# Moving the plain couple of a gated attention and max-out kernel from the end of batch 0 to the start of batch 1

## The chip, the cores and the metric

The kernel runs on one core of a Trainium2 chip. The metric is the device time of one execution in microseconds (us), lower is better. Engines: PE is TensorE, DVE is VectorE, ACT is ScalarE, POOL is GpSimd (it issues the plain loads and most stores), SP is SyncE (it issues the transposing DMAs).

## The reference

Eight batches of 3072 tokens; `u` and `v` have 256 columns, `z` has 64. The output of the first half is the input `x` of the second.

```
scores = (1/S) * z @ z.T                  # per batch, symmetric
attn   = max(scores, 0) ** 2
x      = u * (attn @ v)
out    = max(x @ w1, x @ w2) @ w_out      # 1024 hidden columns
```

## The kernel before

**Tiles.** The 3072 rows of a batch are 24 tiles of 128, six groups of four tiles. `A[b, g, k]` is the block of attn between group g and group k: 128 partitions x 2048 bf16, 512 KB, in one of 28 slots. Two groups are a couple, so a batch has couples 0, 1, 2; the program numbers couples through the batches: i = 2 is batch 0's last couple, i = 3 batch 1's first, i = 4 batch 1's second.

**Scores.** A score pair (`score_pair`, L204) is two matmuls of 64 rows (L218), two Relus on ACT (L231) and a square on DVE (L237, L239); two pairs fill one block. attn is symmetric, so only blocks with k >= g are computed; the block (k, g) is made from (g, k) by `mirror` (L268): one transposing DMA on SP (L270). `z` comes transposed in `zT`: `load_z` (POOL, L136), two copies on DVE (L143), a transposing DMA on SP (L144, `turn_z`). `u` comes by `load_u` (POOL, L188) and is transposed by `turn_u` (SP, L194).

**attn @ v.** The four groups of batch 0 that come first (couples 0 and 1) are done one by one (L286). From i = 2 a couple's work is a list of steps of two matmuls (L898), one on each half of PE's rows, with score pairs of later blocks spread between the steps. A couple is done in one of two ways:

- *Plain*: 96 steps; every matmul reads a block of attn and `v` as they are. `PLAIN_COUPLES` names the couple and the order of its three block columns o.
- *By 7 products* (a Strassen form): 84 steps. It needs sums of attn blocks beforehand, for each o of `SUPERS[c]`: S1 = A21 + A22 (L338), S2 = S1 - A11 (L342), S3 = A11 - A21 (L346), and once per batch and o four sums of `v` pieces (`combine_v`, L174 to L177, one of them in place), all on DVE. Products P1 and P6 come first (steps 0 to 11, the first three o's in turn, four steps each), then P7 beside X11 (steps 12 to 23). P6 reads S2, P7 reads S3.

A11, A12 are the blocks of the couple's first group g, A21, A22 those of g + 1. For batch 0's last couple (groups 4, 5) and o = 0 that is A21 = A[0,5,0], A22 = A[0,5,1]: both are mirrors.

**Second half.** `ff` (L443) does the max-out part of one group: hidden products (L448), then output products (L462, L471), stores from POOL (L484). After the steps of couple i, `second(i - 1, ...)` runs `ff` for the two groups of the couple before; while PE does that, a list of tasks is issued on the other engines: the gates (L432, `x = u * ...` of the couple that has just ended) and, ahead of a couple by 7 products, its sums. The sequence of PE is therefore: steps of i = 2, ff of couple 1, steps of i = 3, ff of couple 2, and so on; the `ff` of couple 0 stands ahead of i = 2.

**Order of the queues.** All engines run the program's order, written by hand; no instruction of POOL or SP waits for a "step" of PE as such: it waits only for its data and its buffer, and for what stands ahead of it on its engine. For i = 2, 3, 4 there are plans of their own (L847 to L870): at which step loads and transposes are put into the queues. In batch 0 the mirrors of groups 0 and 1 into groups 3 to 5 are held back (list `later`) and issued during groups 1 to 3; SP's last seven mirrors ahead of i = 2 are, in order, those that make (5,2), (4,0), (4,1), (4,3), (5,0), (5,1), (5,3), and behind them stands the transpose of z(1), piece 1.

Of the kernel before, what the change touches and what calls it, by code (L numbers as in the profile page):

```python
# [11 lines left out]
def kernel(  # L12
# [23 lines left out]
    G = 4  # L36
    GW = G * P
    NG = NT // G
# [4 lines left out]
    NSLOTS = 28  # L43
    AFTER = mybir.DependencyInfo(mybir.DependencyClass.Sync, mybir.DependencyReason.DATA)
    PLAIN = 4
    PLAIN_COUPLES = {2: (2, 1, 0)}
    DIRECT = ((0, 5, 4),)
    KEEP = 5, 2
    SUPERS = (1, 0, 2), (2, 1, 0), (0, 2, 1)
# [18 lines left out]
    def by_tile(x):  # L68
        return x.rearrange("(p t) d -> p t d", t=NT)
# [35 lines left out]
    def z_at(b, t):  # L105
        piece, k = divmod(t, 2 * G)
        return (NC * b + piece) % 4 * 2 * G + k
# [32 lines left out]
    def turn_z(b, piece):  # L140
        t = zpool.tile([P, 2 * G, 2, dqk], bf16, name="zd")
        for h in range(2):
            nc.vector.tensor_copy(t[:, :, h, :], zn[b, piece])  # L143
        nc.sync.dma_start_transpose(  # L144
            zT[:, ds(z_at(b, piece * 2 * G), 2 * G), :], t.rearrange("p t h d -> p (t h d)")
        )
# [20 lines left out]
    def combine_v(b, piece):  # L167
        w = vp[b, piece]
        b11, b12 = w[:, 0:G, 0:P], w[:, 0:G, P:D]
        b21, b22 = w[:, G : 2 * G, 0:P], w[:, G : 2 * G, P:D]  # L170
        t = tpool.tile([P, 3, G, P], bf16, name="vt")
        t1, t2, t3, t4 = vt[b, piece] = b12, t[:, 0], t[:, 1], t[:, 2]
        return [
            lambda: nc.vector.tensor_sub(t3, b22, b12),  # L174
            lambda: nc.vector.tensor_sub(t1, b12, b11),
            lambda: nc.vector.tensor_sub(t2, b22, t1),
            lambda: nc.vector.tensor_sub(t4, b21, t2),  # L177
        ]
# [5 lines left out]
    def load_u(b, g):  # L184
        un[b, g] = unat.tile([P, G, D], bf16, name="un")
        step = 2 if b or g > 1 else G
        for k in range(0, G, step):
            nc.gpsimd.dma_start(  # L188
                out=un[b, g][:, ds(k, step), :], in_=by_tile(u[b])[:, ds(g * G + k, step), :]
            )  # L190
# [10 lines left out]
    A = {}  # L201
# [66 lines left out]
    def mirror(b, g, blk):  # L268
        t = Block(turned=True)
        nc.sync.dma_start_transpose(  # L270
            t.ap.rearrange("p (k r) -> p k r", r=P), A[b, g, blk].ap
        )
        A[b, blk, g] = t
        A[b, g, blk].release(after=COOL)
# [220 lines left out]
    pairs, pair_at = [], {}  # L495
# [17 lines left out]
    per_batch = (len(pairs) - 2 * len(DIRECT)) // B  # L513

    done = 0
# [39 lines left out]
    def need(b, g, n):  # L555
        most = pair_at[b, g, 2 * g]
        for t in range(n + 1):
            if t // G >= g:
                most = max(most, pair_at[b, g, t // 2] + 1)
        return most  # L560

    with tc.manual_schedule():
# [50 lines left out]
        for i in range(PLAIN):  # L613
            b, g = groups[i]
# [3 lines left out]
            for slot, (n, dc) in enumerate(steps_of(i)):  # L618
                tick += 1
                k = need(b, g, n)  # L620
# [16 lines left out]
                if i in (1, 2) and n in (5, 8):  # L637
                    k = n // 8
# [55 lines left out]
        def second(i, tasks, sums=None):  # L694

            b, c = couples[i]
            tasks = list(tasks)
            places = {(1, 0): 1, (1, 3): 1, (2, 0): 1, (2, 1): 1, (2, 2): 1, (2, 3): 1}

            def hook(stage, n):  # L700
                for _ in range(places.get((stage, n), 0)):
                    if tasks:
                        tasks.pop(0)()

            nonlocal tick
            for q in range(2):
                g = 2 * c + q
                ff(b, g, xTs.pop((b, g)), hook=hook)
                tick += 32
            while tasks:  # L710
                tasks.pop(0)()

        def prepared(i, gates):

            b, c = couples[i]
            for o in range(NC):
                assert all(
                    pair_at[b, min(q, k), 2 * max(q, k) + 1] < done
                    for q in (2 * c, 2 * c + 1)
                    for k in (2 * o, 2 * o + 1)  # L720
                ), (i, done)
            for x in list(to_mirror):
                if x[0] == b and x[2] // 2 == c:
                    to_mirror.remove(x)
                    mirror(*x)
            if i in PLAIN_COUPLES:
                return {}, list(gates)
            tasks = []
            for o in SUPERS[c]:
                if (b, o) not in vt:  # L730
                    tasks += combine_v(b, o)
            forms, sums = prepare(b, c)
            first, *others = [x[:2] for x in sums]
            tasks = gates[:KD] + first + gates[KD:] + tasks + sum(others, [])
            return forms, tasks + [x[2] for x in sums]

        b, g = groups[PLAIN - 1]
        sums = drain(acc, range(KD), copy=nc.vector.tensor_copy)
        forms, tasks = prepared(PLAIN // 2, gate(b, g, sums))
        second(  # L740
            PLAIN // 2 - 2,
            [lambda: turn_z(1, 2)]
            + tasks
            + [lambda: None] * 3
            + [lambda g=g: load_u(0, g) for g in (4, 5)],
        )

        for i in range(PLAIN // 2, len(couples)):
            b, c = couples[i]
            q1, q2 = 2 * c, 2 * c + 1  # L750
            target = min(2 * len(DIRECT) + (b + 1) * per_batch + (-6, 8, 22)[c], len(pairs))
            steps, ends, marks, waits = steps_of_couple(
                b, c, forms, supers=PLAIN_COUPLES.get(i)
            )
# [7 lines left out]
            for f in forms.values():  # L762
                for name, n in (("A11", 1), ("A12", 2), ("A21", 1), ("A22", 1), ("S1", 1)):
                    f[name].quota = 2 * G * n
            plain = i in PLAIN_COUPLES
            if plain:
                for q in (q1, q2):
                    for k in range(NG):
                        A[b, q, k].quota = 4 * G
            for pair in steps:  # L770
                for x in pair:
                    left[x[0]] = left.get(x[0], 0) + 1
# [74 lines left out]
            if i == 2:  # L847
                plan = [
                    (1, turn_u, 0, 4),
                    (4, turn_u, 0, 5),  # L850
                    *((17 + 8 * k, load_v, 1, k // 2, k % 2 * G, G) for k in range(6)),
                ]
            if i == 3:
                plan = [
                    (2, load_u, 1, 0),
                    (6, load_u, 1, 1),
                    (14, load_z, 2, 0),
                    (18, load_z, 2, 1),
                    (22, turn_u, 1, 0),
                    (26, turn_u, 1, 1),  # L860
                    (66, turn_z, 2, 0),
                    (len(steps), load_u, 1, 2),
                    (len(steps), load_u, 1, 3),
                ]
# [11 lines left out]
            for s, pair in enumerate(steps):  # L876
                while halves_done and halves_done[0][0] <= s:
                    _, name, mm = halves_done.pop(0)
                    relays[name] = nc.scalar.nop()
                    tc.add_manual_dep(relays[name].ins, mm.ins.name, AFTER, reason="half done")  # L880
                tick += 1
                flush(tick)
                mirror_ready((b, c), KEEP[s > 36])
                asked += len(at_step.get(s, ()))
                while asked and len(due) < 3 and (
                    at_hand() or pairs[done][2] % 2 or len(steps) - s < 8 * asked
                ):
                    emit_pair(wait=8)
                    asked -= 1
                for do in events.get(s, ()):  # L890
                    do()
                for half, (name, w, blk, j) in enumerate(pair):
                    rows = ds(half * R, R)
                    if name not in acc:
                        acc[name] = acc_tile((PLAIN_BANK if plain else BANK)[name])
                    a = blk()
                    left[name] -= 1
                    mm = nc.tensor.matmul(  # L898
                        a.out(acc[name]),
                        w()[rows],  # L900
                        a.moving(rows, j),
                        start=name not in opened,
                        stop=left[name] == 0,
                    )
                    opened[name] = True
                    if (s, half) in marks:
                        halves_done.append((s + (2 if plain else G), marks[s, half], mm))
                    if (s, half) in waits:
                        relay = relays[waits[s, half]]
                        tc.add_manual_dep(mm.ins, relay.ins.name, AFTER, reason="half done")  # L910
                    a.quota -= 1
                    if not a.quota:
                        a.release()
# [11 lines left out]
            if i + 1 < len(couples):  # L925
                forms, tasks = prepared(i + 1, gates)
            else:
                tasks = gates
            second(i - 1, tasks)
        b, c = couples[-1]  # L930
# [31 lines left out]
```

## Time and profile before

| | us |
|---|---|
| median of 7 runs (lowest, highest) | 918.12 (913.64, 923.65) |
| the profiled execution, its own time | 915.91 |
| its span, first to last instruction | 914.1 |
| ff of couple 0 | 68.1 to 83.9 |
| i = 2, plain, with 22 score pairs | 83.9 to 109.4 |
| ff of couple 1 | 109.4 to 125.4 |
| i = 3, by 7 products, with 14 pairs | 125.4 to 146.3 |
| ff of couple 2 | 146.3 to 162.0 |
| i = 4, by 7 products, with 14 pairs | 162.0 to 185.4 |
| the same couple of the next batch (i = 7) | 274.8 to 295.5 |

Times in views are from the span's start. A line of groups or of the timeline has the engine, the source line, the operation, what it writes and reads, and how often; brackets give idle time before it and what ended it. In the waits, the numbers are total us, times, and the longest.

### The profile page before, as it was taken

What the parts mean: (1) busy time and instruction counts of PE and PEld (TensorE: products, weight loads), DVE (VectorE), ACT (ScalarE), POOL (GpSimd) and SP (SyncE); (2) the same over time, 40 slices, a digit from 0 to 9 for tenths busy, and PEclk for the clock granted to TensorE, in tenths of its full rate; (3) what the DMA queues carried; (4) which work ended last, traced back from release to release, by engine and by line L of the source; (5) the groups of instructions that cost most, each with busy time, mean ns of one, the idle gap of its engine ahead of it and who ended that gap; (6) DMA issues with size and microseconds to landing.
All of it is one profiled execution on the core that took longest, in us unless ns stands there. A gap on an engine that the chain in (4) does not pass through costs nothing.

```text
span 914.1 us, 19379 instructions
## 1 busy us (share of the span) xinstructions
PE 899.8 (98%) x7478; PEld 519.3 (57%) x7526; DVE 722.8 (79%) x1094; ACT 602.0 (66%) x1192; POOL 160.7 (18%) x303
## 2 busy tenths in 40 slices
PE   9899999899999999999999999999999999999998
PEld 4456465464565655655556656566465564655655
DVE  6582689778997799887997979979799788995640
ACT  7787966567666676666666666766766667673445
POOL 4102021211202121111213022030220212101000
PEclk9999999999999999999999999999999999999999
DMA  9999999999999896999979998799988989987201
GB/s 180 178 191 201 119 209 173 149 171 165 186 170 148 176 185 127 181 173 157 188 126 200 157 164 174 130 186 170 163 175 138 193 158 173 163 156 147 74 24 69
DMA packets 396556, 145.60 MB, mean 159 GB/s; under 512 B 361904, under 2 KB 387632, under 8 KB 396464
## 3 DMA queue, kind: packets, MB, share of 16 engines
q1 hardware_dynamic: 359040, 91.79, 64.8%
q0 software_dynamic: 37424, 52.58, 32.6%
q8 instruction: 58, 0.95, 0.4%
q14 instruction: 34, 0.28, 0.1%
HBM read 59.77 MB, written 25.17 MB: 93 GB/s over the span
## 4 chain that ended last, share of the span: by engine, by line
PE 95%; DMA 3%; DVE 1%; issue 1%; ACT 0%; ACTq 0%
PE acc L898 43%; PE o_ps L471 18%; PE d_ps L448 18%; PE s_ps L218 7%; PE o_ps L462 5%; PE acc L286 3%; DMA zT<-zd 2%; DMA blk<-blk 1%; DVE blk L239 0%; PE acc L591 0%; PE tpz L125 0%; PE w2o_ps L680 0%; ACT r_sb L231 0%; DVE w_sb L663 0%; DVE xT L432 0%
## 5 line engine op out<-in xcount | busy, mean ns | idle before, releaser
L898 PE MATMUL acc<-blk,v_sb 64*128 64x512 bf16 x2208 | 450.5, 376 | 0.0
L231 ACT ACTIVATE r_sb<-s_ps 128x512 bf16<-128x512 f32 (+3 forms) x672 | 336.0, 559 | 126.5 <-PE s_ps L218 82.9
L898 PE MATMUL acc<-blk,vt 64*128 64x512 bf16 x1512 | 364.1, 376 | 0.0
L898 PEld LDWEIGHTS <-v_sb 64*128 64x128 bf16 x2208 | 176.3, 94 | 135.3 <-issue 5.7
L239 DVE TENSOR_TENSOR blk<-r_sb 128x1024 bf16<-128x1024 bf16 x257 | 172.4, 688 | 93.9 <-ACT r_sb L231 93.2
L455 ACT ACTIVATE g_sb<-d_ps 128x512 bf16<-128x512 f32 x384 | 193.3, 630 | 28.2 <-PE acc L898 17.7
L471 PE MATMUL o_ps<-w_out_sb,g_sb 128*128 128x256 bf16 x1536 | 175.5, 273 | 0.0
L898 PEld LDWEIGHTS <-vt 64*128 64x128 bf16 x1512 | 139.2, 94 | 62.2
L448 PE MATMUL d_ps<-xT,w_sb 128*128 128x512 bf16 x720 | 167.6, 379 | 2.6 <-issue 0.2
L471 PEld LDWEIGHTS <-g_sb 128*128 128x128 bf16 x1536 | 150.3, 98 | 17.4
L483 ACT COPY o_sb<-o_ps 128x512 f32<-128x512 f32 (+1 forms) x98 | 56.3, 577 | 132.5 <-PE o_ps L471 132.5
L484 POOL DMA_DIRECT2D out_dram<-o_sb x88 | 48.1, 547 | 529.6 <-ACT o_sb L483 529.6
L775 DVE TENSOR_TENSOR h_sb<-h_sb,acc 128x512 f32<-128x512 f32 x168 | 109.4, 682 | 28.3 <-ACT h_sb L779 20.9
L218 PE MATMUL s_ps<-zT 64*128 64x512 bf16 (+3 forms) x676 | 126.6, 359 | 2.5 <-DMA zT<-zd 2.5
L448 PEld LDWEIGHTS <-w_sb 128*128 128x128 bf16 x768 | 73.3, 98 | 89.4 <-issue 9.5
L342 DVE TENSOR_TENSOR blk<-blk,blk 128x2048 bf16<-128x2048 bf16 x63 | 77.2, 1225 | 5.6 <-DMA blk<-blk 3.5
L338 DVE TENSOR_TENSOR blk<-blk,blk 128x2048 bf16<-128x2048 bf16 x63 | 76.7, 1218 | 0.0
L790 DVE TENSOR_TENSOR blk<-blk,blk 128x2048 bf16<-128x2048 bf16 x63 | 76.6, 1218 | 0.0
L346 DVE TENSOR_TENSOR blk<-blk,blk 128x2048 bf16<-128x2048 bf16 x63 | 73.3, 1218 | 2.9 <-DMA blk<-blk 2.9
L188 POOL DMA_DIRECT2D un<-in_u_dram x94 | 50.5, 563 | 87.2 <-DMA uT<-un 84.2
L432 DVE SCALAR_TENSOR_TENSOR xT<-h_sb,uT 128x512 bf16<-128x512 f32 x96 | 62.0, 684 | 4.3 <-PE o_ps L462 4.3
L237 DVE TENSOR_TENSOR blk<-r_sb 128x512 bf16<-128x512 bf16 (+3 forms) x162 | 46.5, 324 | 19.7 <-ACT r_sb L231 18.6
(48 smaller groups left out, 358.8 us busy)
## 6 DMA issues: line engine op xcount, KB each, us to landing
out_dram<-o_sb POOLq DMA_DIRECT2D x88, 256.0 KB, 3.7
un<-in_u_dram POOLq DMA_DIRECT2D x92, 128.0 KB, 5.2
v_sb<-in_v_dram POOLq DMA_DIRECT2D x74, 128.0 KB, 5.7
blk<-blk SPq DMA_TRANSPOSE x240, 4.9
v_sb<-in_v_dram POOLq DMA_DIRECT2D x11, 256.0 KB, 13.3
zn<-in_z_dram POOLq DMA_DIRECT2D x21, 128.0 KB, 4.3
out_dram<-o_sb SPq DMA_DIRECT2D x6, 256.0 KB, 2.0
blk<-in_moe_w_dram POOLq DMA_DIRECT2D x2, 512.0 KB, 7.5
```

The source lines that it names most:

```text
L218: nc.tensor.matmul(s_ps[h][:, lo[h] :], zT[rows, z_at(b, blk * G + tiles[h]), :], zT[rows, q + lo[h] // P : q + G, :].rearrange("p t c -> ...
L231: nc.scalar.activation(o, s, AF.Relu)
L239: nc.vector.tensor_mul(a[:, k : k + 2, :], r, r)
L338: nc.vector.tensor_add(*alike(f["S1"], f["A21"], f["A22"]))
L342: nc.vector.tensor_sub(*alike(f["S2"], f["S1"], f["A11"]))
L346: nc.vector.tensor_sub(*alike(f["S3"], f["A11"], f["A21"]))
L448: nc.tensor.matmul(d_ps, w15_sb[:, kc, ts(nb, P)], xT[:, kc, :], start=(kc == 0), stop=(kc == KD - 1),)
L455: nc.scalar.activation(g_sb[:, nb, :], d_ps, AF.Relu)
L471: nc.tensor.matmul(o_ps[t // 2][:, t % 2, :], g_sb[:, nb, ts(t, P)], w_out_sb[:, nb, :], start=False, stop=(nb == KF - 1 and t % 2 == 1),)
L775: nc.vector.tensor_add(out, a, b_)
L790: nc.vector.tensor_sub(f["A12"].ap, f["A12"].ap, f["S2"].ap)
L898: mm = nc.tensor.matmul(a.out(acc[name]), w()[rows], a.moving(rows, j), start=name not in opened, stop=left[name] == 0,)
```

## The change

Couple i = 2 is done by 7 products, with 14 score pairs beside it (`ahead`), and i = 3 plain, with 22. The sums for i = 2 are issued as tasks during the `ff` of couple 0, and batch 0's `combine_v` with them; batch 1's `combine_v` moves from the `ff` ahead of i = 3 to the one ahead of i = 4. `load_u(0, 4)` and `load_u(0, 5)` go from the end of the `ff` of couple 0 to its second and fourth task. `turn_z(1, 2)` goes from that `ff` to step 40 of i = 2. Four of the six loads of v(1) are put at steps 26 to 56 of i = 2 instead of 17 to 41, the last two behind its end instead of at 49 and 57. u(1, 0) and u(1, 1) are loaded and turned some 20 steps sooner. A plain couple may start while the blocks of its last column are still to come.

```diff
-    PLAIN_COUPLES = {2: (2, 1, 0)}
+    PLAIN_COUPLES = {3: (0, 1, 2)}
...
-                ), (i, done)
+                ) or (i in PLAIN_COUPLES and o == PLAIN_COUPLES[i][-1]), (i, done)
...
-        second(
-            PLAIN // 2 - 2,
-            [lambda: turn_z(1, 2)]
-            + tasks
-            + [lambda: None] * 3
-            + [lambda g=g: load_u(0, g) for g in (4, 5)],
-        )
+        for n, g in ((1, 4), (3, 5)):
+            tasks[n] = lambda do=tasks[n], g=g: (do(), load_u(0, g))
+        second(PLAIN // 2 - 2, tasks)
...
-            target = min(2 * len(DIRECT) + (b + 1) * per_batch + (-6, 8, 22)[c], len(pairs))
+            ahead = 14 if i == 2 else (-6, 8, 22)[c]
+            target = min(2 * len(DIRECT) + (b + 1) * per_batch + ahead, len(pairs))
...
             if i == 2:
                 plan = [
                     (1, turn_u, 0, 4),
                     (4, turn_u, 0, 5),
-                    *((17 + 8 * k, load_v, 1, k // 2, k % 2 * G, G) for k in range(6)),
+                    (40, turn_z, 1, 2),
+                    *((26 + 10 * k, load_v, 1, k // 2, k % 2 * G, G) for k in range(4)),
+                    (70, load_u, 1, 0),
+                    (76, load_u, 1, 1),
+                    (len(steps), load_v, 1, 2, 0, G),
+                    (len(steps), load_v, 1, 2, G, G),
                 ]
             if i == 3:
                 plan = [
-                    (2, load_u, 1, 0),
-                    (6, load_u, 1, 1),
+                    (1, turn_u, 1, 0),
+                    (4, turn_u, 1, 1),
                     (14, load_z, 2, 0),
                     (18, load_z, 2, 1),
-                    (22, turn_u, 1, 0),
-                    (26, turn_u, 1, 1),
                     (66, turn_z, 2, 0),
                     (len(steps), load_u, 1, 2),
                     (len(steps), load_u, 1, 3),
                 ]
```

What is left out of the diff counts the uses of a plain couple's blocks when they are first read instead of ahead of the couple.

## The prediction

> **What bounds the kernel now.** I read the page first (busy time, then the chain that ended last), then the waits, then a table by stage.
>
> ```profile
> PE 899.8 (98%) x7478; PEld 519.3 (57%) x7526; DVE 722.8 (79%) x1094; ACT 602.0 (66%) x1192; POOL 160.7 (18%) x303
> ...
> PE 95%; DMA 3%; DVE 1%; issue 1%; ACT 0%; ACTq 0%
> ```
>
> PE is busy 98% of the span and is 95% of the chain, so time can only be won where PE stands still or by less work on PE. The waits of PE show the two places where it stands still for long:
>
> ```profile
> PE acc L286 <- DMA blk<-blk: 2.8, 1, 2.8
> PE s_ps L218 <- DMA zT<-zd: 2.5, 1, 2.5
> ```
>
> The first is at 37.2 us, ahead of everything that the change touches. The second is in i = 4. The table by stage (length, then busy time of PE, PEld, DVE, ACT, POOL with counts, then PE's clock, DMA share, GB/s) finds nothing else:
>
> ```profile
> 68.10:83.90 15.80, 15.70 (x114) 10.91 (x116) 2.61 (x6) 10.08 (x20) 3.80 (x7) 1.00 1.12 198
> 83.90:109.40 25.50, 25.50 (x237) 11.35 (x236) 14.54 (x21) 24.23 (x45) 3.77 (x7) 1.00 1.36 131
> 109.40:125.40 16.00, 15.89 (x114) 10.90 (x116) 15.43 (x25) 10.72 (x22) 1.65 (x3) 1.00 1.18 215
> 162.00:185.40 23.40, 20.87 (x198) 10.59 (x198) 17.64 (x37) 13.60 (x30) 5.38 (x10) 1.00 1.30 146
> 274.80:295.50 20.70, 20.70 (x198) 11.68 (x197) 14.82 (x32) 13.52 (x30) 5.34 (x10) 1.00 1.24 151
> ```
>
> The plain couple with its 22 pairs runs without a hole (25.50 of 25.50), though ACT is busy for 24.23 of it. i = 4 takes 2.7 us more than its sister in the next batch (last line). The ff of couple 1 is 0.2 longer than later ones (15.9 against 15.7). **So from 68 us on there are 2.7 us to win at most.**
>
> **PE's work.** Nothing is added or removed: i = 2 loses 24 matmuls and 8 pairs (16 matmuls), i = 3 gains the same. A stage by 7 products with 14 full pairs takes 21.3 us elsewhere (i = 5, 201.1 to 222.4), the plain one 25.5; their sum stays. Cost 0. Beside the plain i = 3 stand ACT's 44 Relus, as now beside i = 2 without a hole. Cost 0.
>
> **The sums for i = 2: the main term.** In the ff of couple 0 DVE now does 2.61 us of work. It gets S1, S2, S3 for three o's and batch 0's 12 sums of v. The same list stands ahead of i = 6, a couple by 7 products without late inputs:
>
> ```profile
> 225.88 1.22 DVE L338 TENSOR_TENSOR blk<-blk,blk 128x2048 bf16<-128x2048 bf16 x1
> ...
> 228.28 1.28 DVE L432 SCALAR_TENSOR_TENSOR xT<-h_sb,uT 128x512 bf16<-128x512 f32 x2
> 229.48 0.41 DVE L174 TENSOR_TENSOR vt<-v_sb 128x512 bf16<-128x512 bf16 x1
> ...
> 235.87 1.23 DVE L342 TENSOR_TENSOR blk<-blk,blk 128x2048 bf16<-128x2048 bf16 x1
> ...
> 239.41 3.49 DVE L346 TENSOR_TENSOR blk<-blk,blk 128x2048 bf16<-128x2048 bf16 x3
> 242.81 0.68 DVE L239 TENSOR_TENSOR blk<-r_sb 128x1024 bf16<-128x1024 bf16 x1
> ```
>
> From the first S1 to the end of the last S3 it takes 242.81 - 225.88 = 16.93, less two gates (1.20) that i = 2 doesn't have there: **15.7 us in one row**, and DVE takes it in order. There the last S3 is needed at step 20: 24 slots (20 steps, 4 pairs) of 0.217 us (21.26 us / 98 slots of i = 5) after 238.1, at 243.3; it has 0.5 us to spare.
>
> When can the first S1 of i = 2 start? It reads A[0,5,0] and A[0,5,1]. The second is SP's sixth mirror of the last seven, the one at 71.7 (that line of SP's, then its time to landing):
>
> ```profile
> L270 SPq DMA_TRANSPOSE blk<-blk x1: 2422/2422/2422, 71.7 to 71.7; - x1
> ...
> DMA to landing us min/median/max: 5.0/5.0/5.0
> ```
>
> It lands at 76.8. The two gates ahead (L432) end at 73.9, so DVE then waits, and all sums behind wait with it. Last S3: 76.8 + 15.7 = 92.5. PE wants it at step 20: 83.85 + 5.2 = 89.1. **PE waits 3.4 us** (1.8 of it at step 4, where S2 of the second o ends 9.9 after the first S1). In the kernel before, the plain order (2, 1, 0) read these mirrors last.
>
> **The u loads run into those mirrors.** u(0, 4) and u(0, 5), four loads of 128 KB, wait only for buffers that are free by 60.5, and stand right behind POOL's z load of 64.25. So they start near 65 instead of at 77.5, beside the mirrors of 63 to 77. Below: nothing, if SP's pace and not the DMA engines hold these mirrors; a gain is excluded, as SP's first 25 entries are the same in both kernels. Above: the same four loads now stand beside two zT transposes, with two stores, and these land after
>
> ```profile
> DMA to landing us min/median/max: 9.1/9.7/10.4
> ```
>
> instead of the 4.4 median of zT: up to 6.0 later. The loads are half of those bytes (512 KB, the stores 512 KB), which would make 2.7; the loads turn fp32 into bf16 and so read twice as much, and I take 3.5, between the two. **+3.5 (0 to 6.0).**
>
> PE's hole at step 4 becomes 5.3 us. After the 2.83 us hole at 37.2 the granted clock was 0.70 in 40 to 42 and 0.50 in 42 to 44 us, some 3.2 us at half speed, worth 1.6. But DVE's chain paces PE up to step 20 anyway: **+0.5 (0 to 1.6)**. The Trainium skill, "TensorE: Matmul & The Clock Gate", "What's actually happening", speaks against the change here: half rate after an idle window of about 3.4 us, windows running free of the kernel. By that rule a 1.8 us hole is safe and a 5.3 us one may not be; the row shows that 2.83 us was enough, so the row decides, and by the page alone the term would be the same or nothing.
>
> **The stall in i = 4.** PE wants piece 1 of z(2) 17.5 us into the couple (179.5 - 162.0). Its transpose was issued 4.3 in and took 15.9 to land, behind two uT transposes and beside the loads of v(2) and u. The issue comes 1.1 later in the changed kernel: batch 1's 12 sums of v (5.1 us) move into the ff of couple 2, where S3 now ends 18.3 after its start and in the ff with such sums 20.1. That delay itself costs PE nothing, as the ff of couple 1 shows: S3 ended at 129.5 and PE had no hole. The two uT transposes can go earlier, since SP has fewer mirrors piled up (8 blocks fewer beside i = 2). Landing after 10.4 (the slowest zT beside loads above): 15.8 in, no wait, gain 2.5. After 15.9 again: 21.3 in, wait 3.8, loss 1.3. I take **-2.0 (-2.5 to +1.3)**, nearer the first, because the pile ahead is smaller.
>
> **The rest.** u(0, 4) and u(0, 5) land before 80 and their transposes start before the v loads; now these landed 16 and 22 us late, the second at 110.1, and ff of couple 1 was 0.2 long: **-0.2**. z(1)'s last turn (two copies of 0.29 and a DMA) leaves SP at 79.4 for step 40; its first reader is a pair of i = 3: 0, with 15 us of ff as cover; without cover it would be a wait like the 2.5 above. Four of the six v(1) loads don't move at all: POOL doesn't wait for steps, they still stand right behind the stores of ff 0, at 85.4. The last two wait for i = 2's last matmul, since they overwrite batch 0's piece; the stores of ff 1 queue behind them, but the first is ready 7 us later (75.3 against 68.1 in ff 0), and their reader is step 64 of i = 3, some 30 us on. Their landings now are 13 to 17 us: 0. A plain i = 3 reads its last column at step 64; those 8 pairs are done by step 40: 0.
>
> **Sum:** 3.4 + 3.5 + 0.5 - 2.0 - 0.2 = **+5.2 us**. On the profiled execution's own 915.9 (span 914.1 and 1.8 around it) that is 921.1. The median of the runs is 2.2 higher, 918.1; what they have more is not in this profile, and I add the same 5.2 to it: **923.3 us**.
>
> **Rivals.**
>
> *The loads don't hurt* (delay 0 to 1, no loss of clock). For it: SP's mirrors go out back to back from 58.5, so SP may be the limit. Against: they take 1.8 to 3.6 us of SP each, and the 3.6 is the one beside the z load. 3.4 + 0.5 - 2.5 - 0.2 = +1.2: 919.3.
>
> *Not slower: the mirror is there in time.* Without other traffic SP issues a mirror in 1.94 (189.9 us). Six at that pace from 58.5 put the sixth at 68.2, landing at 73.2, ahead of the gates' end at 73.9, the point from which DVE never waits. Then S3 ends at 89.6, PE waits 0.6: 0.6 - 2.5 - 0.2 = -2.1: 916.0. Against: six in a row were slower in the profile, and the loads come on top.
>
> *Worse: the slow stretch moves.* From 85 to 110 us, beside v loads, uT took 16 and 22 us. If loads and mirrors near 66 fall into that, the delay is the full 6.0 and the clock's 1.6, and i = 4 keeps its stall: 3.4 + 6.0 + 1.6 = +11.0: 929.1. Against: it needs the larger v loads.
>
> *It doesn't do what it says*: that holds for four of the v loads, as shown; its price is in the sums.
>
> **Chances.** Forecast 0.62, loads that don't hurt 0.22, mirror in time 0.09, worse 0.07. 0.5% is 4.6 us, about what a measurement of this kernel can tell from no change. Of the forecast's 0.62, 0.50 lies above it; with the worst case, slower 0.57. Faster needs the second rival and more: 0.04. Same: the remaining 0.39. Range: from the second rival, 916.0, to all upper ends, 3.4 + 6.0 + 1.6 + 1.3 = 12.3: 930.4; I write 916 to 930.
>
> **What would show it.** The profile after: PE waiting for DVE (L342, L346) in the first 20 steps of i = 2; DVE idle from 73.9 until a blk DMA lands, near 80; the u loads near 65; i = 2 at 27 to 29 us instead of 21.3; i = 4 at 20.7 to 21.3 instead of 23.4. I am wrong if DVE's first S1 starts before 75, if the mirrors keep their times beside the u loads, or if i = 4 keeps its wait.

## The result, and the profile after

The changed kernel took 922.95 us (median of 26 runs, 921.08 to 931.17) against 917.0 for the kernel before on the same chips (61 runs, 909.18 to 932.14): a ratio of 1.0087, with a 95% interval of 1.0066 to 1.0107. The forecast was 923.3, made on a median of 918.12. The profiled execution took 923.88 (span 922.1), 8.0 us more than the one of before.

First the page: the busy times, and the chain that ended last, which now has DVE in it with 4%.

```profile
PE 904.3 (98%) x7478; PEld 527.7 (57%) x7526; DVE 727.4 (79%) x1106; ACT 601.4 (65%) x1192; POOL 161.0 (17%) x303
...
PE 92%; DVE 4%; DMA 2%; issue 1%; ACT 0%; ACTq 0%; DVEq 0%
```

The waits (total us, times, longest) give the place. The zT wait of 2.5 is gone; in its stead PE waits for S2, and DVE for a mirror.

```profile
DVE blk L338 <- DMA blk<-blk: 6.6, 2, 5.4
...
PE acc L286 <- DMA blk<-blk: 4.4, 1, 4.4
PE acc L896 <- DVE blk L342: 4.1, 1, 4.1
```

The table by stage, with the same columns as before (ff of couple 0, i = 2, ff of couple 1, i = 3 and, after the ff of couple 2, i = 4):

```profile
70.30:86.00 15.70, 15.60 (x112) 10.84 (x111) 6.47 (x11) 10.09 (x20) 1.65 (x3) 1.00 1.19 206
86.00:114.90 28.90, 24.77 (x197) 11.47 (x196) 26.14 (x38) 16.02 (x30) 5.87 (x11) 0.88 1.24 144
114.90:130.60 15.70, 15.60 (x111) 10.87 (x112) 4.92 (x9) 9.71 (x19) 1.65 (x3) 1.00 1.17 131
130.60:156.00 25.40, 25.40 (x238) 19.02 (x236) 14.53 (x27) 22.53 (x46) 3.75 (x7) 1.00 1.25 170
171.80:193.40 21.60, 21.48 (x198) 11.01 (x198) 20.27 (x39) 13.50 (x30) 5.34 (x10) 1.00 1.21 178
```

The plain stage has no hole in its new place (25.40 of 25.40). i = 2 takes 28.9, where the same couple of batch 1 (i = 5) takes 21.26: an excess of 7.6, partly hole (24.77 busy of 28.90), partly clock (0.88). From i = 5 on the two traces agree. Measured between starts of PE's stages, the way from ff of couple 0 to i = 5 grew from 132.97 to 138.85: **+5.9**. The other 2.1 of the 8.0 lie ahead of ff of couple 0 (70.28 against 68.12), where PE's instructions are the same in both kernels: the wait for a mirror at L286 was 4.4 instead of 2.8, with more half clock behind it. That is spread from run to run, not the change: in the profiles of after and of the versions built on it, ff of couple 0 begins anywhere between 64.3 and 77.1.

DVE's timeline shows the chain (start, length, instruction, idle time before it):

```profile
74.81 1.29 DVE L432 SCALAR_TENSOR_TENSOR xT<-h_sb,uT 128x512 bf16<-128x512 f32 x2 [3.73 <-PE o_ps L462]
81.47 1.22 DVE L338 TENSOR_TENSOR blk<-blk,blk 128x2048 bf16<-128x2048 bf16 x1 [5.37 <-DMA blk<-blk]
...
90.26 1.23 DVE L342 TENSOR_TENSOR blk<-blk,blk 128x2048 bf16<-128x2048 bf16 x1
...
93.79 3.49 DVE L346 TENSOR_TENSOR blk<-blk,blk 128x2048 bf16<-128x2048 bf16 x3
97.20 1.89 DVE L239 TENSOR_TENSOR blk<-r_sb 128x1024 bf16<-128x1024 bf16 x3
```

The gates end at 76.1, DVE stands idle for 5.37 us, and the first S1 starts when the mirror has landed. From there to the end of the last S3 it is 97.20 - 81.47 = 15.73. The mirror is the one that SP issued at 76.6:

```profile
L270 SPq DMA_TRANSPOSE blk<-blk x1: 1923/1923/1923, 76.6 to 76.6; - x1
...
  DVE blk L338: 5.4, 1
...
DMA to landing us min/median/max: 4.8/4.8/4.8
```

Its own 4.8 us to landing is ordinary; what made it late is that SP came to it late, since the mirrors ahead of it were slow: (4,3), issued at 67.7, took 9.1 us to land, against 4.6 in before. The DMA view of 60 to 80 us, for before and then for after, shows what lay beside them (packets, MB, share of the 16 engines' time; software_dynamic is POOL's queue):

```profile
q1 hardware_dynamic: 14390, 3.63, 104.5%
q0 software_dynamic: 259, 0.54, 11.0%
```

```profile
q1 hardware_dynamic: 12642, 3.19, 93.5%
q0 software_dynamic: 720, 0.66, 26.0%
```

The u loads add 15% of 20 us to POOL's share, 3.0 us of all engines, and the transposes move 12% less in the same time. That this is the cause is left to e12.

Last, PE's first instruction after the hole, and the clock behind it (the column after the five engines):

```profile
91.53 0.58 PE L896 MATMUL acc<-blk,vt 64*128 64x512 bf16 x1 [4.05 <-DVE blk L342]
```

```profile
90.00:94.00 4.00, 2.39 (x12) 0.87 (x13) 3.93 (x5) 0.96 (x2) 1.06 (x2) 0.62 1.16 117
94.00:98.00 4.00, 4.00 (x22) 1.59 (x23) 4.00 (x5) 1.21 (x3) 0.00 (x0) 0.53 1.29 64
```

By the clock records it was half from 90.97 to 97.80, 6.83 us.

### The profile page after: what moved, and what is told of

The parts are those of the page before. It is cut to its first block, busy times and chain, and to the rows that moved or that the text cites. A ratio compares the mean times of both kernels' runs of the same rounds, so it can differ in the third digit from the quotient of the medians.

```text
span 922.1 us, 19389 instructions
## 1 busy us (share of the span) xinstructions
PE 904.3 (98%) x7478; PEld 527.7 (57%) x7526; DVE 727.4 (79%) x1106; ACT 601.4 (65%) x1192; POOL 161.0 (17%) x303
## 4 chain that ended last, share of the span: by engine, by line
PE 92%; DVE 4%; DMA 2%; issue 1%; ACT 0%; ACTq 0%; DVEq 0%
PE acc L896 44%; PE o_ps L471 17%; PE d_ps L448 17%; PE s_ps L218 7%; PE o_ps L462 4%; PE acc L286 3%; DMA blk<-blk 2%; DVE blk L338 1%; DVE blk L342 1%; DVE blk L239 0%; DVE xT L432 0%; PE acc L591 0%; DVE vt L174 0%; DVE v_sb L175 0%; DVE vt L176 0%
## 5 line engine op out<-in xcount | busy, mean ns | idle before, releaser
L896 PEld LDWEIGHTS <-v_sb 64*128 64x128 bf16 x2208 | 183.1, 94 | 134.1 <-issue 14.3
L218 PE MATMUL s_ps<-zT 64*128 64x512 bf16 (+3 forms) x676 | 133.0, 361 | 0.2 <-DVE zT L130 0.2
L783 DVE TENSOR_TENSOR blk<-blk,blk 128x2048 bf16<-128x2048 bf16 x63 | 76.6, 1218 | 0.1
L346 DVE TENSOR_TENSOR blk<-blk,blk 128x2048 bf16<-128x2048 bf16 x63 | 73.3, 1219 | 1.7 <-DMA blk<-blk 1.7
L218 PEld LDWEIGHTS <-zT 64*128 64x128 bf16 x676 | 39.3, 95 | 37.2 <-issue 1.3
```

The source lines that it names most:

```text
L218: nc.tensor.matmul(s_ps[h][:, lo[h] :], zT[rows, z_at(b, blk * G + tiles[h]), :], zT[rows, q + lo[h] // P : q + G, :].rearrange("p t c -> ...
L346: nc.vector.tensor_sub(*alike(f["S3"], f["A11"], f["A21"]))
L783: nc.vector.tensor_sub(f["A12"].ap, f["A12"].ap, f["S2"].ap)
L896: mm = nc.tensor.matmul(a.out(acc[name]), w()[rows], a.moving(rows, j), start=name not in opened, stop=left[name] == 0,)
```

## The experiments

**Theory.** The end of i = 2 is set by the landing of mirror (5,1) and the sums queued behind it on DVE, and u loads beside the mirrors make that landing later. Let D be the time from the start of ff of couple 0 to that landing. Then the excess of i = 2 over 21.26 should be D + (sums behind it) - 20.9, where 20.9 = 15.7 of ff + 5.2 of 24 slots; clock comes on top. **Rivals:** the amount of DVE work in the ff; the half clock; loads that are hidden anyway.

The profiles, in one table (us; the lateness is the formula's):

| kernel | D | sums behind | lateness | excess measured | half clock in i = 2 |
|---|---|---|---|---|---|
| after | 11.1 | 15.7 | 5.9 | 7.6 | 6.83 |
| e1, order of o | 16.4 | 8.2 | 3.7 | 3.9 | none |
| e2, u later | 6.9 | 15.7 | 1.7 | 2.0 | none |
| e3, PE kept busy | 12.5 | 15.7 | 7.3 | 7.6 | none |
| e4, v sums first | 11.1 | 10.6 | 0.8 | 1.5 | none |
| e8, PE delayed | 9.5 | 15.7 | 4.3 | 5.5 | 3.41 |
| e12, u behind the stores | 9.1 | 15.7 | 3.9 | 4.3 | 3.41 |

**e1: the order of the block columns.** Batch 0's last couple takes o = 2 first, whose sums don't need mirror (5,1).

```diff
-        for o in SUPERS[c]:
+        for o in (2, 0, 1) if b == 0 else SUPERS[c]:
```

> The changed kernel, with the sums of batch 0's last couple in the order o = 2, 0, 1 instead of 0, 2, 1, so that DVE begins with a block column that needs no mirror. Theory (DVE waits for a late mirror with everything behind it): the first S1 starts right behind the gates, 4.5 us after the first output product of that ff or some 6 us after the ff's start, the last S3 ends 15.7 us later, 21.5 after the ff's start, and is wanted at 20.9: i = 2 takes 21.3 + 0.6 = 21.9 us (21.3 to 23) instead of 28.9, with no stretch at half clock; the execution gets 6 to 7 us shorter than the changed kernel, some 916. Rival (the sheer amount of DVE work, 12 more sums and 9 block sums, doesn't fit into this ff): the amount is the same, i = 2 stays at 27 to 29.

918.74 us, ratio 1.0055 (1.0017 to 1.0094). i = 2 fell to 25.18, in full clock, though (5,1) landed 16.4 us after the start of ff: fewer sums stood behind it. That is over the 21.3 to 23 expected, since the mirror landed 5.3 later after that start than in after; the lateness accounts for 3.7 of the excess of 3.9. But i = 4 took 24.88: the transpose of z(2), piece 1, took 14.4 us to land, and PE waited 2.4 for it. The gain in i = 4 isn't safe.

**e2: the u loads later**, beside the seventh and eighth task.

```diff
-        for n, g in ((1, 4), (3, 5)):
+        for n, g in ((6, 4), (7, 5)):
```

> The changed kernel, with the loads of u(0,4) and u(0,5) put back to where the kernel before has them (behind the first two stores of ff 0). Theory (these loads delay the mirrors by some 2.4 us): the mirror that the first S1 waits for lands 8.7 us after the start of ff 0 instead of 11.1, the hole before step 20 is 3.5 instead of 6.0, and with a shorter hole the half clock lasts 0 to 3.4 us instead of 6.8: i = 2 takes 24.8 to 26.5 instead of 28.9. Rival (the mirrors go at SP's own pace, the later landing was the z load or chance): i = 2 stays at 28 to 29.

919.97 us, 1.0069 (1.0018 to 1.0119). i = 2 took 23.25, less than the 24.8 to 26.5 expected, but this profile had a hole of 11.4 us in its opening, so that D was 6.9 partly for that reason. It can't price the loads alone; e12 does.

**e3: PE kept busy in the hole**, by 18 matmuls that nothing reads, ahead of step 4 of i = 2.

```diff
+                if i == 2 and s == 4:
+                    fill = mm_psum.tile([P, GW], fp32, name="fill", tag="mm")
+                    for n in range(18):
+                        nc.tensor.matmul(
+                            fill, w15_sb[:, 0, :P], w15_sb[:, 1, :GW], start=True, stop=True
+                        )
```

> The changed kernel, with 18 matmuls of 128 x 512 that nobody reads on PE ahead of step 4 of i = 2, 3.9 us of work, so that PE isn't idle while it waits there. Theory (1.7 us of the 7.6 us that i = 2 is too long are half clock after the idle hole): no granted clock under 0.9 in i = 2, and i = 2 takes 27.0 to 27.4 instead of 28.9. Rival (DVE's chain sets the pace all along, the clock costs nothing): 28.7 to 29.

922.61 us, 1.0116 (1.0068 to 1.0164). The clock of i = 2 stayed full, and the stage was no shorter, since the mirror landed 1.4 us later than in after:

```profile
85.60:114.50 28.90, 26.59 (x215) 12.57 (x216) 27.46 (x42) 15.96 (x30) 5.90 (x11) 1.00 0.96 151
```

So my expected length was missed, with the measured one in the rival's range, and the lateness explains it (7.3 of 7.6). Half clock isn't the main cause.

**e4: the v sums first.** The 12 sums of v go ahead of the gates and of S1, into the time in which DVE waits for the mirror. The amount of DVE work is unchanged.

```diff
-            tasks = gates[:KD] + first + gates[KD:] + tasks + sum(others, [])
+            if b == 0:
+                tasks = tasks + gates + first + sum(others, [])
+            else:
+                tasks = gates[:KD] + first + gates[KD:] + tasks + sum(others, [])
```

> The changed kernel, with batch 0's 12 sums of v taken ahead of the gates and of the block sums, into time in which DVE waits. The mirror stays as late as it is. Theory: behind the mirror stand 15.7 - 5.1 = 10.6 us of sums instead of 15.7; the last S3 ends 0.9 us later than PE wants it, so i = 2 takes 22.2 (21.8 to 23) instead of 28.9, at full clock. Rival (the amount of DVE work): the amount is the same, so 27 to 29.

919.74 us, 1.0071 (1.0029 to 1.0113); i = 2 at full clock:

```profile
85.30:108.00 22.70, 21.90 (x198) 10.72 (x196) 21.24 (x29) 15.96 (x30) 5.89 (x11) 1.00 1.29 161
```

With D as in after, 11.1, moving 5.1 us of work from behind the mirror to ahead of it took 6.2 us from i = 2. The last S3 ended 4.7 sooner after the start of ff (22.3 against 27.0); the remaining 1.5 fits the half clock that isn't there. The rival "amount of DVE work" falls: what counts is what stands behind the mirror. The lateness of 0.8 in the table is short of the excess of 1.5 because DVE then met the next mirror, (5,3), which landed at 86.02:

```profile
86.04 1.22 DVE L338 TENSOR_TENSOR blk<-blk,blk 128x2048 bf16<-128x2048 bf16 x1 [0.34 <-DMA blk<-blk]
```

The profiled execution, 916.18, is the second fastest of the ten. Against after (922.95) the median fell by 3.2 only, so the whole gain isn't in every execution.

**e5: all three together**, the edits of e1, e2 and e4.

> The changed kernel with three moves together: batch 0's 12 sums of v ahead of everything, the order o = 2, 0, 1, and the u loads back behind the first stores of ff 0. Behind the mirror (5,1) stand 8.2 us of sums (S1 and S2 of two o's, three S3), and the mirrors have no u loads beside them. Theory: with that mirror landing 6 to 12 us after the start of ff 0, the last S3 ends at 14 to 20, ahead of the 20.9 at which PE wants it; i = 2 takes 21.3 to 22, at full clock. Rival (part of the loss has another cause in i = 2, such as the score pairs or the products themselves): i = 2 over 22.5.

919.99 us, 1.0034 (0.9993 to 1.0076): a miss, for i = 2 was expected at 21.3 to 22. This profile had no hole in its opening (ff of couple 0 began at 64.31), and i = 2 took 35.1:

```profile
DVE blk L338 <- DMA blk<-blk: 11.8, 1, 11.8
PE acc L899 <- DVE blk L342: 11.2, 1, 11.2
```

The mirror is now the last one, (5,3): issued at 73.5, it landed at 91.2. The DMA view of these 17.7 us, and below it that of the last mirror of e11 (72.7 to 81.0), which took 8.3:

```profile
q0 software_dynamic: 1059, 1.88, 70.7%
q1 hardware_dynamic: 3995, 1.01, 52.7%
```

```profile
q1 hardware_dynamic: 4170, 1.05, 94.4%
q0 software_dynamic: 160, 0.52, 20.9%
```

The same bytes of transposes (about 1 MB) took 17.7 us where POOL's queue (stores, u loads, v loads) had 71% and 8.3 us where it had 21%. A packet of POOL's queue is 1.88 MB / 1059 = 1775 bytes there and took 0.707 x 17.7 x 16 / 1059 = 0.19 us; one of the transposes is 253 bytes and took 0.037 us. The Trainium skill, "DMA: Bandwidth & Descriptors", "Queues, rings and completion order", says that an engine takes its queues in turn, one packet from each. Over the whole stretch the counts are not one to one (1059 against 3995), and the transposes had 53% of the engines' time. From 88 to 92 us they are:

```profile
q0 software_dynamic: 237, 0.48, 83.0%
q1 hardware_dynamic: 241, 0.06, 25.0%
```

There the transposes moved 0.06 MB in 4 us, where e11's moved about 0.5 MB in as long (1.05 MB in 8.3 us). So beside loads a transpose can get far less than half of the engines, as it would if an engine took one long and one short packet in turn. That the packets of this view are those of the page, no run here shows.

**e6: the kernel before, with the transpose of z(2), piece 1, turned sooner** (at step 76 of i = 3 instead of step 10 of i = 4), to see that stall alone.

```diff
+                    (76, turn_z, 2, 1),
...
-                    (10, turn_z, 2, 1),
```

> The kernel before with one edit: piece 1 of z(2) is turned at step 76 of i = 3 instead of step 10 of i = 4, so its transpose stands ahead of the two uT transposes and of the loads of v(2). Theory (the 2.5 us in i = 4 are that one transpose behind starved transposes): PE's wait in i = 4 is gone, i = 4 takes 20.7 to 20.9 instead of 23.3. Rival (something else is as late, the score pairs' blocks or v): i = 4 stays over 22.

914.49 us, 0.9989 (0.9945 to 1.0033). i = 4 took 20.71, its stall gone. The profiled execution was a long one of this kernel (926.47), and shows what the profile of before didn't: the kernel before can have the collision of e5 too, here after a quick opening (ff of couple 0 at 64.57):

```profile
PE s_ps L218 <- DMA zT<-zd: 13.3, 1, 13.3
```

Mirror (5,3) took 18.6 us to land and the transpose of z(1), piece 1, 20.7; i = 2 took 42.0.

**e7: e5 and the turn of e6.**

> The changed kernel with the three moves of the run before the last and, in addition, piece 1 of z(2) turned at step 76 of i = 3. Theory: i = 2 at 21.3 to 22 and i = 4 at 20.7 to 21, whatever the loads do in that run; from the start of ff 0 to the start of i = 5 it takes 130.3 to 131.5 us, against 133.0 in the kernel before and 138.9 in the changed one; the median is 0 to 3 us under that of the kernel before. Rival: the gains move a wait to the next couples, and this stretch stays at 133 or more.

922.99 us, 1.0052 (1.0009 to 1.0095). A miss as well: the collision of e5 came again (i = 2: 35.5), and the way from ff of couple 0 to i = 5 took 144.65 where 130.3 to 131.5 was expected. i = 4 took 20.71.

**e8: after, with PE delayed by 28 unread matmuls (6.05 us) ahead of ff of couple 0.** If the landing sets the end of i = 2, the delay costs little; if PE's work does, it costs 6.

```diff
+        delay = mm_psum.tile([P, GW], fp32, name="delay", tag="mm")
+        for n in range(28):
+            nc.tensor.matmul(delay, w15_sb[:, 0, :P], w15_sb[:, 1, :GW], start=True, stop=True)
```

> The changed kernel, with 28 matmuls of 128 x 512 that nobody reads on PE right ahead of ff 0: 6.05 us of additional work on PE. Theory (the end of i = 2 is set by the time at which a mirror lands, not by PE): the mirrors land when they did, so i = 2 gets 5 to 7 us shorter and the whole stays within 2 us of the changed kernel: 921 to 925. Rival (PE's own work sets the end): 6 us more, 929.

920.99 us, 1.0028 (0.9994 to 1.0063): with 6 us more work on PE it was no longer than after (1.0087). i = 2 took 26.80, as the table has it, only 2.1 less than in after, where 5 to 7 less was expected: in this profile ff of couple 0 began at 70.15 with the delay in it, so its opening was some 6 us quicker than that of after. The median carries this test, not the profile.

**e9: the kernel before with the same delay.**

> The kernel before with the same 28 matmuls ahead of ff 0. Theory: nothing in i = 2 waits for the mirrors there, so all 6.05 us show: median of the kernel before plus 5 to 7 us, i = 2 unchanged at 25.6. Rival (such work is hidden in both kernels): under 3 us more.

919.9 us, 1.0027 (0.9985 to 1.0068). The lowest run rose by 5.3 (911.13 to 916.43), the median by 1.1 only: I had expected 5 to 7. In this profile the u loads were issued at 80.2, after (5,3) had landed at 78.7, and i = 2 had no hole (25.57). That suggests that in the kernel before, too, a quick PE runs its stores and u loads into SP's last transposes, and that the delay took away such waits while it added its own time. e11 tests that. It also means that e8 by itself doesn't set after apart: most of the delay stays out of the median in both kernels.

**e10: no load beside any of these transposes.** e5's order and v sums, the u loads behind the four stores of ff, v(1) behind u(1, ·), and the turn of e6.

```diff
-        for n, g in ((1, 4), (3, 5)):
-            tasks[n] = lambda do=tasks[n], g=g: (do(), load_u(0, g))
-        second(PLAIN // 2 - 2, tasks)
+        second(PLAIN // 2 - 2, tasks + [lambda g=g: load_u(0, g) for g in (4, 5)])
...
-                    *((26 + 10 * k, load_v, 1, k // 2, k % 2 * G, G) for k in range(4)),
-                    (70, load_u, 1, 0),
-                    (76, load_u, 1, 1),
+                    (62, load_u, 1, 0),
+                    (64, load_u, 1, 1),
+                    *((66 + 4 * k, load_v, 1, k // 2, k % 2 * G, G) for k in range(4)),
```

> The changed kernel with batch 0's supers prepared in the order 2, 0, 1, batch 0's twelve v sums ahead of its gates and block sums, u(0,4) and u(0,5) loaded behind the four stores of ff 0 instead of ahead of them, the first four v(1) loads behind the two u(1,.) loads, and zT(2,1) turned at step 76 of i=3. It computes the whole result. Theory (mirrors starve when loads run beside them, and the end of i=2 is the landing of its last mirror plus the sums behind it): no load lies beside the mirrors of i=2 or beside zT(1,1) any more, so the last mirror lands within 13 to 14.5 us of the start of the mirror before last four, i=2 takes 21.3 to 22.5 us, i=4 20.7, and the median is 908 to 916. Rival (the transposes starve beside the stores just as well, or the u(0,.) transposes behind the later loads come too late): a wait of 5 us or more stays in ff 0, i=2 or i=3, and the median stays at 917 or above.

919.39 us, 1.0036 (0.9995 to 1.0077). In i = 2, (5,1) landed 14.45 us after (4,1) started, within the 13 to 14.5 expected, but (5,3), beside the stores, took 8.2 to land; DVE's last S1 waited for it, and the stage took 23.0 instead of 21.3 to 22.5. A slow transpose came back in another place, i = 4, which took 27.1:

```profile
DVE blk L784 <- DMA blk<-blk: 4.9, 1, 4.9
PE acc L897 <- DVE h_sb L769: 4.2, 1, 4.2
```

A mirror issued at 161.1, just ahead of a store, a z load and four v loads, took 14.4 us to land. The median was missed, on the rival's side.

**e11: the kernel before, with the u loads behind the four stores of ff of couple 0.**

```diff
-            + [lambda: None] * 3
+            + [lambda: None] * 20
```

> The kernel before, with u(0,4) and u(0,5) loaded behind the four stores of ff 0 instead of ahead of them; nothing else. Theory (in a part of the executions of the kernel before, the last mirror of i=2 and zT(1,1) lie beside the u loads and PE waits for them; the delay of 6 us cost only 1.1 us in the median because it moved them apart): i=2 takes 25.6 to 26 us in the profile and the median falls by 2 to 5 us below the kernel before. Rival (the u loads are not what starves them, or the later u loads make the u transposes late): the median is within 1.5 us of the kernel before, or above it.

910.68 us (12 runs, 908.97 to 919.12) against 915.9 (23 runs, 909.21 to 928.9); the ratio is 0.9973 (0.9942 to 1.0003), which just includes no difference. 10 of its 12 runs lie under 913.1, and 8 of the 23 of before. Its profile (span 907.6) has ff of couple 0, i = 2 and i = 4 without a hole:

```profile
64.20:79.90 15.70, 15.70 (x114) 10.86 (x112) 2.61 (x6) 10.09 (x20) 1.64 (x3) 1.00 1.11 194
79.90:105.50 25.60, 25.60 (x238) 11.41 (x236) 14.54 (x21) 24.23 (x45) 5.86 (x11) 1.00 1.19 198
158.10:178.80 20.70, 20.70 (x197) 11.68 (x196) 15.09 (x34) 13.52 (x30) 5.35 (x10) 1.00 1.29 157
```

Its opening was as quick as those of e5, e6 and e7, and PE met no late transpose; (5,3) took 8.3 us to land, beside stores only. This is the version with the lowest median of all.

**e12: after, with the u loads behind the stores**, nothing else: the price of the loads by itself.

```diff
-        for n, g in ((1, 4), (3, 5)):
-            tasks[n] = lambda do=tasks[n], g=g: (do(), load_u(0, g))
-        second(PLAIN // 2 - 2, tasks)
+        second(PLAIN // 2 - 2, tasks + [lambda g=g: load_u(0, g) for g in (4, 5)])
```

> The changed kernel with u(0,4) and u(0,5) loaded behind the four stores of ff 0, where the second experiment put them beside the seventh and eighth task; nothing else differs from the changed kernel. With the kernel before in the same form (loads behind the stores) it is the price of the change without loads beside its mirrors. Theory: the last mirror lands 12.6 to 14.3 us after the mirror before last four starts, no more than 9.5 us after ff 0 begins, and PE waits landing + 15.7 - 20.9 us: i=2 takes 23 to 26 us, at full clock or with one half-clock window, i=4 20.7 to 21.6; median 915 to 920, that is 4 to 9 us above the kernel before in that form. Rival (the loads beside the mirrors cost nothing in the changed kernel, or something else does): i=2 stays at 28 us or more, and the median at 922 to 924.

917.52 us (914.8 to 918.74), 1.0005 (0.9973 to 1.0037) against the kernel before. (5,1) lands 12.6 us after (4,1) started, against 17.3 in after, DVE waits 3.4 instead of 5.4, and i = 2 takes 25.5:

```profile
83.40:108.90 25.50, 23.28 (x197) 13.88 (x196) 24.22 (x34) 15.93 (x30) 7.99 (x15) 0.93 1.10 177
```

```profile
DVE blk L338 <- DMA blk<-blk: 3.4, 1, 3.4
PE acc L894 <- DVE blk L342: 2.2, 2, 2.1
```

e11 is the kernel before in the same form. From ff of couple 0 to i = 5 the two profiles take 134.68 and 130.37: without loads beside the mirrors the change still costs 4.3, which is the excess of i = 2.

## Why the prediction was right, point by point

The path was the foretold one: a late mirror, DVE's sums queued behind it, PE waiting in the first steps of i = 2. The total fits better than its terms do, and part of that is luck.

- **The sums for i = 2 (+3.4): confirmed.** The chain took 15.73 us (15.7 foretold, read from i = 6), and S2 of the second o ended 91.45 - 81.47 = 9.98 after the first S1 (9.9). In e12, where no load hinders the mirrors, the lateness is 3.9 and the excess 4.3, where the prediction had 3.4 + 0.5. e4, which takes sums out from behind the mirror, brings the excess down to 1.5.
- **The loads beside the mirrors (+3.5): confirmed as a cause, with 2.4 of it reaching PE.** By SP's own time, from the start of mirror (4,1) to the landing of (5,1), it was 12.6 to 15.0 in nine profiles without u loads beside it (before, e2, e5, e6, e7, e9, e10, e11, e12; in e5, e6 and e7 the first of them start some 3 us ahead of the landing), and 16.8 to 19.3 in the five with (after, e1, e3, e4, e8): about 4; in the profiled pair 13.6 and 17.3. But D grew by 2.4 only (8.65 to 11.1), since PE's ff began 2.2 later in after. So the lateness was 5.9 where the prediction had 3.4 + 3.5 = 6.9. Between after and e12, i = 2 differs by 28.89 - 25.56 = 3.3: 2.0 of lateness, the rest fits the clock. The medians, not taken side by side, differ by 5.4 (922.95 and 917.52); where the other 2.1 lie isn't shown. My reason (bytes, with fp32 counted twice) was too simple: the DMA rows of e5 point to time per packet on the same engines.
- **The clock (+0.5, bound 1.6): the term that was too small.** The hole of 4.2 was followed by 6.83 us of half clock, two periods of 3.41, so that PE, not DVE, paced the steps up to 20: PE never waited for S3 (L346), which I had also named. 4.2 + 6.83 / 2 = 7.6 is the whole excess; at full clock it would have been the lateness, 5.9 (6.1 by the end of the last S3), as it was in e3. So the clock's net price was about 1.6, the upper bound. It differed from run to run: e3 had none, and in e12 3.41 us of half clock cost at most 0.4, since DVE was late in any case. That the lateness came out 1.0 smaller and the clock 1.1 larger than foretold, so that the excess fits (7.6 against 7.4), is luck.
- **The stall in i = 4 (-2.0): the number came out, the path didn't.** i = 4 went from 23.32 to 21.56: -1.76. The transpose of z(2), piece 1, landed 16.0 us into the couple, and 15.8 was foretold; but that was to be an issue 5.4 in and 10.4 to landing, and it was an issue 12.2 in and 3.8 to landing. The issue came some 8 us later than in before (4.2 in), not 1.1, since the two uT transposes ahead of it went later, not earlier. SP's rows, for before and then for after (the couple starts at 162.04 and 171.83):

```profile
162.76 3.42 SPq L194 DMA_TRANSPOSE uT<-un  x2
166.28 6.51 SPq L144 DMA_TRANSPOSE zT<-zd  x1
```

```profile
176.42 7.48 SPq L194 DMA_TRANSPOSE uT<-un  x2
184.01 1.74 SPq L144 DMA_TRANSPOSE zT<-zd  x1
```

That the two sums agree is luck. Nor is it shown that the change takes the stall away: e9 and e11, which leave i = 4 as in the kernel before, took 20.71, and e1, with the change, 24.88. It comes and goes in both kernels. The 0.85 that after's i = 4 has over 20.71 fits that stage's own sums, after DVE waited 1.24 us at 169.1 for a mirror.
- **ff of couple 1 (-0.2): confirmed**, 15.92 to 15.75. The plain i = 3 ran without a hole in every profile of the changed kernel and its versions (25.25 to 25.4).
- **Together:** from ff of couple 0 to i = 5 +5.9 (+5.2 foretold), in the medians 922.95 - 917.0 = +6.0. Of the 0.7 too much, 0.2 each lies in i = 2 and in i = 4; the rest are differences of about 0.1 in terms that the prediction put at 0. The forecast of 923.3 lies closer, within 0.4, because its base, a median of 7 runs, was 1.1 above that of all 61: luck again.
- **The rivals.** "The loads don't hurt" falls with e12. "The mirror is in time" falls with the timeline: the first S1 starts at 81.47, the gates end at 76.1; even without the loads (e12) it starts at 76.84, behind the gates' end at 73.5. "The slow stretch moves" didn't happen in after, but it is real: e5, e6, e7.
- **What I didn't see:** the kernel before isn't one time but a mixture. After a quick opening its own stores and u loads can fall on the last transposes, and the gain is lost: e6's profile shows it, with 146.78 us from ff of couple 0 to i = 5, and the times of e9 and e11 fit. "2.7 us to win at most" was read from one execution. In after the end of i = 2 hangs on the mirrors, as its timeline, e4 and e12 show, and 6 us more work on PE didn't lengthen its median (e8), though before hides most of such a delay too (e9). The quick half of after's runs lies close together, at 921.1 to 923.0, and that of before's between 909.2 and 917.0. That fits, but these runs have no traces that would show it for each.

Left open: why the wait at L286 in the opening differs between 0 and 11.4 us from profile to profile.

## What to carry to other kernels

When a stage by products that need sums is moved to a place where its inputs come last, price it as landing of the last input plus all that is queued behind it on the in-order engine, against the slot in which it is read; first move out from behind that input what doesn't need it. Keep loads of another queue away from a run of dependent DMA transposes, and put them behind work that comes later (here: the stores); then ask what they will lie beside next, for moving them starved another transpose in e10. A profile of one execution may show the kind side of a race between queues: look at the spread of the runs before you take its stages as the rule.

## What was not expected of the hardware

A DMA transpose of 512 KB that took 4.4 to 6.9 us in the profile of before took 17.7, 18.6 and 18.8 beside loads and stores of POOL's queue (e5, e6, e7), and SP stood behind it.

Apart from the first and the last microseconds, half clock came in stretches of 3.41, 6.83, 13.65 and 17.07 us, multiples of one period. Where a trace has two such stretches, they begin a whole number of periods apart (51.20 us or 15 periods in after, 47.79 us or 14 in e12), so the periods run on whatever PE does. The length of a hole doesn't decide: one of 2.1 us in e12 was followed by half clock, one of 2.5 us in i = 4 of before wasn't. When the time in which no matmul is recorded is added up period by period, all 14 traces agree. A period at full clock with 2.07 us or more of such time (2.07 in e12, 2.16 in e8, 2.18 in e5) was followed by one at half clock. One with 1.83 us or less (1.83 in e1; the hole of before lies across two, 1.03 and 1.49) was not. A period at half clock was followed by another if PE stood still in it for 0.64 us (after) or more, and by full clock after 0.58 us (e12) or less; so after's hole, which reached 0.6 us into its second period, cost two. The Trainium skill, "TensorE: Matmul & The Clock Gate", "What's actually happening", has the period (3413 ns, running free), which these rows show; its condition of an idle window of about 3.4 us is too strict for the 2.07 us of e12.
